# Sharing softmax exps between ScalarE and VectorE: lending a PSUM bank and waiting for full PV rounds in a planned attention kernel

## The chip, the cores and the metric

The kernel runs on one core of a Trainium2 chip. The metric is the device time of one execution in microseconds. Before the change three runs gave 832.87, 833.47 and 835.27 us, with a median of 833.47 us.

## What is computed

A layer norm of x (2048 rows, 512 wide) feeds multi-query attention with 32 heads of width 16, and beside it a two-matrix SiLU network of width 1792. The SiLU of the network's result gates the attention's result.

```python
xn = _layernorm(x)
q = (xn @ wq).reshape(B, S, 32, 16).transpose(0, 2, 1, 3)
k, v = xn @ wk, xn @ wv                       # one key and value head for all
scores = jnp.einsum("bhqd,bkd->bhqk", q, k) * 16 ** -0.5
o = jnp.einsum("bhqk,bkd->bhqd", softmax(scores), v)
s = o.transpose(0, 2, 1, 3).reshape(B, S, 512) @ wo
h = _silu(xn @ w1)                            # 512 -> 1792
return x + s * _silu(h @ w2)                  # 1792 -> 512
```

## The kernel before

The 2048 x 2048 scores of 32 heads make 2048 slots. A slot is one matmul on TensorE (PE in the profile): 128 keys by 512 queries of one head, into one PSUM bank. The slots are ordered by group `g`: 512 queries of four heads, 64 slots, 32 groups in all. Every slot's scores must go through an exp, and the result meets V in a PV matmul that adds to the bank `OB` of its group.

There are two ways through the exp.

- ScalarE (ACT): a unit of three slots (banks 0 to 2, the wide buffer) or of two (banks 3 and 4, the narrow buffer) is turned into bf16 by one ACTIVATE (L1130) into one of six `pa_sb` buffers. The two buffers take turns. One PV matmul per slot follows (`pa_sb`).
- VectorE (DVE): a slot is turned into bf16 bits by one linear TENSOR_SCALAR out of PSUM (L839, `db_sb`), an exp in which the mantissa is linear. Four such slots make a batch, and five more TENSOR_SCALARs over the whole batch (L871, `ds_sb`) add constants to the bits; the six shifted copies are weighted in V (`v_sb`) and added up by PV. So a DVE slot costs one eviction, five quarters of a shift, and six PV matmuls in place of one. The banks for DVE slots are 5 and 7 (`POOL_BANKS`), which also serve the projections (`jobs`: q, the network's h and z, and the output w; L390).

TensorE works in two modes. An S phase (`do_S`, L677) fills the next ACT unit and up to two DVE slots: two to four matmuls in different row strips that run at once. All else is in rounds: four matmuls into four column strips at once, either of a job or of PV (`do_pv`, L928). A PV round holds, for each of the four heads, one operand that is ready, and may have fewer than four matmuls.

All of it is put in order before the kernel runs, by a planner in the kernel's own code. It keeps a clock per engine and places instructions at planned costs: a round or an S phase takes `MM` = 216 ns, a change between the two modes `SWITCH` = 105 ns, an exp of n slots 0.8333 * 512 * n + 65 ns, an eviction 620 and a shift 600 ns, and there are fixed latencies between engines. The engines then run these orders as they are, each waiting on semaphores of the others. So a rule of the planner sets the order on every engine. The rules that matter here are:

- `want_d` and `dve_backlog`: an S phase takes DVE slots only while the planned DVE backlog is at most `DVE_LIMIT` = 2500 ns and a pool bank is free; at most one beside a wide unit, at most `D_MAX2` = 2 beside a narrow one.
- `s_phase_ready`: an S phase comes when the banks of the next unit are free; `pe_step` puts rounds in between only as far as they don't make the planned S phase too late for ACT (`act_need`, `S_TOL`).
- `pv_round`: a PV round is issued with whatever is ready.
- The order on DVE goes by priority: evictions have 2, shifts 6.

Of the kernel before, what the change touches and what calls it, by code (L numbers as in the profile page):

```python
# [5 lines left out]
ACT = mybir.ActivationFunctionType  # L6
ALU = mybir.AluOpType
# [14 lines left out]
SHIFT_BETA = -0.603400124  # L22
K = len(SHIFT)

PE, AC, DV, PO, SP, AQ = "PE", "ACT", "DVE", "POOL", "SP", "ACTQ"
ENGINES = (PE, AC, DV, PO, SP)
MM = 216.0
SWITCH = 105.0
INF = float("inf")
DVE_LIMIT = 2500.0  # L30
MARGIN, MARGIN_END = 16, 28
D_MAX2 = 2
S_TOL = 30.0


# [184 lines left out]
def bass_recurrent_scan__grouped_kv_mqa__dense_activation_silu__prompt_kernel(  # L220
# [27 lines left out]
    POOL_BANKS = (5, 7)  # L248
    NPA, NDB, NDS = 6, 4, 2 * (K - 1)
    NQR, NON = 4, 2 * NOC  # L250

    with ExitStack() as es:
# [35 lines left out]
        ps = es.enter_context(nc.psum_tensor([P, 8 * 512], FP32))  # L288
# [9 lines left out]
        pl = Planner()  # L298
# [59 lines left out]
        for j in range(4):  # L358
            a, b = 4 * j, 4 * j + 4
# [264 lines left out]
        nleft = [SLOTS] * NG  # L624
# [4 lines left out]
        st = dict(gA=0, gD=0, gO=0, fill=0, expn=0, assigned=0)  # L629
# [5 lines left out]
        pool_free = list(POOL_BANKS)  # L635
# [16 lines left out]
        def take(g, i):  # L652
            kt = left[g, i].pop(0)
            nleft[g] -= 1
            left_oct[g // 2] -= 1
            st["assigned"] += 1
            return kt
# [29 lines left out]
        def dve_backlog():  # L687
            return sum(t.dur for t in pl.tasks[DV] if all(p.op is not None for p in t.preds)) + max(0.0, pl.clk[DV] - pl.clk[PE])

        def want_d(banks_left=True):  # L690
            if st["assigned"] < 8 or not pool_free:
                return False
            if any(c not in evac_kt or evac_kt[c].op is None for c in range(NC)):
                return False
            if dve_backlog() > DVE_LIMIT:
                return False
            return True
# [39 lines left out]
        class Unit:  # L737
            pass

        def s_phase_ready():  # L740
            ub = st["fill"] % 2
            banks = A_BANKS[ub]
            if len(units) >= 2 and units[-2].exp is None:
                return None
            g = a_group(0)
            if g >= NG:
                return None
            if not all(slot_ok(g, i) for i in range(4) if left[g, i]):
                return None
            r = 0.0  # L750
            for b in banks:
                r = max(r, pl.ready(PE, (), [("ps", b)]))
            i = next(i for i in range(4) if left[g, i])
            r = max(r, pl.ready(PE, s_reads(g, i, left[g, i][0]), ()))
            return r
# [5 lines left out]
            return t  # L761

        def pe_start(t, mode):
            return t + (SWITCH if pl.mode not in (None, mode) else 0.0)

        def do_S(t):
            ub = st["fill"] % 2
            banks = A_BANKS[ub]
            dslots = []
            bt = None  # L770
            avoid = set()
            nd = 0
            if want_d():
                bt = d_batch()
                if bt is not None:
                    need = [i for i in range(4) if i not in bt.slots and left[bt.g, i] and slot_ok(bt.g, i)]
                    need.sort(key=lambda i: -len(left[bt.g, i]))
                    if need:
                        cap = len([b for b in pool_free if pl.ready(PE, (), [("ps", b)]) <= t + 30])
                        nd = min(cap, 4 - len(banks), len(need), 1 if len(banks) == 3 else D_MAX2)  # L780
                        for i in need[:nd]:
                            avoid.add(i)
                            dslots.append((bt.g, i, take(bt.g, i)))
            sl = pick_a(len(banks), avoid)
            if sl is None:
                for (g, i, kt) in dslots:
                    left[g, i].insert(0, kt)
                    nleft[g] += 1
                    left_oct[g // 2] += 1
                    st["assigned"] -= 1  # L790
                return False
            mm = []
            reads, writes = [], []
            for k, (g, i, kt) in enumerate(sl):
                mm.append((banks[k], g, i, kt))
                reads += s_reads(g, i, kt)
                writes.append(("ps", banks[k]))
            dinfo = []
            for (g, i, kt) in dslots:
                fb = [b for b in pool_free if pl.ready(PE, (), [("ps", b)]) <= t + 30]  # L800
                b = fb[0]
                pool_free.remove(b)
                mm.append((b, g, i, kt))
                reads += s_reads(g, i, kt)
                writes.append(("ps", b))
                dinfo.append((b, g, i, kt))
            seen = {}
            for (_, _, i, _) in mm:
                seen[i] = seen.get(i, 0) + 1
            dur = MM * max(seen.values())  # L810
            mm.sort(key=lambda m: 0)

            def emit(pe, mm=tuple(mm)):
                h = None
                for (b, g, i, kt) in mm:
                    h = s_mm(pe, b, g, i, kt)
                return h
            op = pl.place(PE, dur, emit, sorted(set(reads)), writes, t0=max(t, pe_start(pl.clk[PE], "S")))
            pl.mode = "S"
            u = Unit()  # L820
            u.slots, u.banks, u.exp, u.pv, u.s_end = sl, banks, None, len(sl), pl.vis(op, AC)
            u.idx = len(units)
            units.append(u)
            st["fill"] += 1
            for (g, i, kt) in sl:
                tot[g, i] += 1
            if dinfo:
                if not bt.slots:
                    batches.append(bt)
                    db_busy[bt.b] = 4  # L830
                for (b, g, i, kt) in dinfo:
                    bt.slots[i] = kt
                    tot[g, i] += K

                    def placed(pop, b=b, g=g, i=i, kt=kt, bt=bt):
                        pool_free.append(b)
                        pvq[g][i].append((pop, v_lhs(0 + 1, g, kt), db_sb[:, bt.b, i * NQ:(i + 1) * NQ].bitcast(BF16),
                                          [("Db", bt.b, i)] + v_reads(1, kt), ("b", bt)))
                    bt.P[i] = pl.add(Task(DV, 620.0, lambda v, b=b, i=i, bb=bt.b: v.tensor_scalar(  # L839
                        db_sb[:, bb, i * NQ:(i + 1) * NQ], bank(b), 128.0 * LOG2E, 128.0 * SHIFT_BETA + 16256.0,  # L840
                        op0=ALU.mult, op1=ALU.add), [("ps", b)], [("Db", bt.b, i)], 2, on_place=placed))
                if len(bt.slots) == 4:
                    make_shifts()
            return True
# [37 lines left out]
        def pv_round(t):  # L882
            g = st["gO"]
            if g >= NG:
                return None
            if g > 0 and norm.get(g - 1) is None or g > 0 and norm[g - 1].op is None:
                return None
            rb = pl.ready(PE, (), [("ps", OB)])
            if rb > t + 20:
                return ("wait", rb)  # L890
            got = {}
            soon = INF
            for i in range(4):
                for k, ent in enumerate(pvq[g][i]):
                    if ent[3][-1][1:] not in v_ready:
                        continue
                    r = max(pl.vis(ent[0], PE), pl.ready(PE, ent[3], ()))
                    if r <= t + 20:
                        got[i] = k
                        break  # L900
                    soon = min(soon, r)
            if not got:
                return ("wait", soon)
            return ("go", got)

        def do_pv(t, got):
# [156 lines left out]
        def a_pressure():  # L1063
            return sum(1 for b in pa_busy if b)

        def pe_step():
            t = pl.clk[PE]
# [6 lines left out]
            pr = pv_round(t)  # L1074
            tr = tail_round(t)
            col = None
            if pr and pr[0] == "go" and (a_pressure() >= NPA - 2):
                col = ("pv", pr[1])
            elif jr[0] == "go":
                col = ("job", jr[1])  # L1080
            elif pr and pr[0] == "go" and len(pr[1]) >= 3:
                col = ("pv", pr[1])
            elif pr and pr[0] == "go":
                col = ("pv", pr[1])
            elif tr and tr[0] == "go":
                col = ("tail", None)
            if ts is not None:
# [3 lines left out]
                elif col is not None:  # L1091
                    mode = col[1].mode if col[0] == "job" else "C"
# [138 lines left out]
```

## Time and profile before

| What | Value |
|---|---|
| median of three runs | 833.47 us |
| the profiled execution: its time, its span | 833.06 us, 831.3 us |
| ACT busy | 794.5 us, 96% of the span |
| PE busy | 723.5 us, 87% |
| DVE busy | 681.4 us, 82% |
| slots through ACT, through DVE | 1668, 380 |
| ACTIVATEs of three slots, of two | 334, 333 |

The span is from the first to the last instruction. Busy time counts an instant once, also where two instructions of an engine overlap. The chain of work that ended last is followed back from the last instruction, and says which engine the end hung on.

### The profile page before, as it was taken

What the parts mean: (1) busy time and instruction counts of PE and PEld (TensorE: products, weight loads), DVE (VectorE), ACT (ScalarE), POOL (GpSimd) and SP (SyncE); (2) the same over time, 40 slices, a digit from 0 to 9 for tenths busy, and PEclk for the clock granted to TensorE, in tenths of its full rate; (3) what the DMA queues carried; (4) which work ended last, traced back from release to release, by engine and by line L of the source; (5) the groups of instructions that cost most, each with busy time, mean ns of one, the idle gap of its engine ahead of it and who ended that gap; (6) DMA issues with size and microseconds to landing.
All of it is one profiled execution on the core that took longest, in us unless ns stands there. A gap on an engine that the chain in (4) does not pass through costs nothing.

```text
span 831.3 us, 19227 instructions
## 1 busy us (share of the span) xinstructions
PE 723.5 (87%) x8492; PEld 211.9 (25%) x8492; DVE 681.4 (82%) x1159; ACT 794.5 (96%) x743; POOL 17.2 (2%) x47
## 2 busy tenths in 40 slices
PE   3988888888988889999988989888989889898986
PEld 1422222222222222222222222222222222222221
DVE  7678887798797887989988878988878788888882
ACT  1999999999999999999999999999999999999994
POOL 2410000000000000000000000000000000000000
PEclk9999999999999999999999999999999999999988
DMA  9100000000000000000000000000000000000000
GB/s 317 39 14 1 2 2 2 1 2 2 2 1 14 27 15 1 2 2 2 2 1 3 26 26 2 2 1 2 2 2 1 14 27 14 1 2 2 2 1 26
DMA packets 11394, 12.53 MB, mean 15 GB/s; under 512 B 1776, under 2 KB 10736, under 8 KB 11312
## 3 DMA queue, kind: packets, MB, share of 16 engines
q1 hardware_dynamic: 9728, 10.75, 4.0%
q8 instruction: 67, 1.10, 0.5%
q10 hardware_dynamic: 1584, 0.56, 0.3%
q14 instruction: 15, 0.12, 0.0%
HBM read 8.95 MB, written 2.10 MB: 13 GB/s over the span
## 4 chain that ended last, share of the span: by engine, by line
ACT 86%; PE 8%; DVE 4%; POOL 1%; issue 1%; ACTq 0%; DVEq 0%
ACT pa_sb L1130 82%; ACT t_sb L505 3%; PE ps L390 3%; PE ps L928 2%; PE ps L677 2%; DVE ds_sb L871 1%; ACT t_sb L528 1%; DVE db_sb L839 1%; DVE v_sb L334 1%; DVE stats_sb L348 1%; DVE xn_sb L367 0%; PE ps L405 0%; POOL v_sb L462 0%; POOL rstd_sb L363 0%; DVE qt_sb L485 0%
## 5 line engine op out<-in xcount | busy, mean ns | idle before, releaser
L1130 ACT ACTIVATE pa_sb<-ps 128x1536 bf16<-128x1536 f32 (+1 forms) x667 | 782.6, 1475 | 10.6 <-PE ps L677 8.6
L677 PE MATMUL ps<-qt_sb,kt_sb 32*128 32x512 bf16 x2048 | 265.4, 390 | 79.0 <-ACT pa_sb L1130 72.8
L839 DVE TENSOR_SCALAR db_sb<-ps 128x512 uint16<-128x512 f32 x380 | 257.1, 684 | 93.3 <-PE ps L677 92.3
L871 DVE TENSOR_SCALAR ds_sb<-db_sb 128x2048 uint16<-128x2048 uint16 x475 | 307.1, 683 | 2.7
L928 PE MATMUL ps<-pa_sb,v_sb 128*32 128x512 bf16 x1668 | 256.2, 390 | 1.6 <-DVE f_sb L945 1.0
L928 PE MATMUL ps<-ds_sb,v_sb 128*32 128x512 bf16 x1900 | 229.3, 389 | 3.9 <-DVE ds_sb L871 2.3
L677 PEld LDWEIGHTS ps<-qt_sb,kt_sb 32*128 32x128 bf16 x2048 | 65.6, 91 | 345.3 <-ACT pa_sb L1130 318.9
L928 PE MATMUL ps<-db_sb,v_sb 128*32 128x512 bf16 x380 | 124.3, 390 | 2.7 <-DVE f_sb L945 2.3
L928 PEld LDWEIGHTS ps<-pa_sb,v_sb 128*32 128x32 bf16 x1668 | 65.4, 95 | 79.3 <-issue 56.3
L928 PEld LDWEIGHTS ps<-ds_sb,v_sb 128*32 128x32 bf16 x1900 | 58.7, 95 | 72.5 <-DVE ds_sb L871 34.9
L390 PE MATMUL ps<-w_sb,u_sb 128*32 128x512 bf16 x896 | 73.8, 384 | 0.1
L390 PE MATMUL ps<-xnT_sb,w_sb 128*32 128x512 bf16 x896 | 72.2, 388 | 0.5 <-DVE u_sb L507 0.5
L505 ACT ACTIVATE t_sb<-ps 128x512 bf16<-128x512 f32 x56 | 47.8, 853 | 0.0
L507 DVE SCALAR_TENSOR_TENSOR u_sb<-t_sb,ps 128x512 bf16<-128x512 bf16 x56 | 38.1, 681 | 10.3 <-ACT t_sb L505 9.9
L928 PEld LDWEIGHTS ps<-db_sb,v_sb 128*32 128x32 bf16 x380 | 31.0, 95 | 18.4 <-DVE f_sb L945 5.8
L945 DVE STREAM_TRANSPOSE f_sb<-ps 128x512 f32<-128x512 f32 x32 | 22.7, 708 | 15.0 <-PE ps L928 15.0
L390 PEld LDWEIGHTS ps<-xnT_sb,w_sb 128*32 128x32 bf16 x896 | 19.0, 95 | 29.8 <-issue 20.2
L390 PEld LDWEIGHTS ps<-w_sb,u_sb 128*32 128x32 bf16 x896 | 18.0, 94 | 29.0 <-issue 21.7
L390 PE MATMUL ps<-wo_sb,on_sb 128*32 128x512 bf16 x256 | 21.0, 424 | 0.5 <-DVE u_sb L507 0.5
L390 PE MATMUL ps<-xnT_sb,wq_sb 128*32 128x512 bf16 x256 | 20.4, 398 | 0.0
L405 PE MATMUL ps<-ident,xn_sb 128*128 128x128 bf16 x64 | 7.1, 289 | 12.8 <-DVE xn_sb L367 12.8
L485 DVE TENSOR_SCALAR qt_sb<-ps 128x512 bf16<-128x512 f32 x16 | 11.0, 688 | 6.6 <-PE ps L390 6.6
(39 smaller groups left out, 155.3 us busy)
## 6 DMA issues: line engine op xcount, KB each, us to landing
w_sb<-in_B_w_dram SPq DMA_DIRECT2D x2, 1792.0 KB, 14.0
xr_sb<-in_A_x_dram SPq DMA_DIRECT2D x16, 128.0 KB, 2.2
out_dram<-ob_sb SPq DMA_DIRECT2D x16, 128.0 KB, 1.7
ds_sb<-in_A_x_dram SPq DMA_DIRECT2D x3, 512.0 KB, 9.2
ds_sb<-in_A_x_dram SPq DMA_DIRECT2D x2, 256.0 KB, 3.3
wq_sb<-in_A_wq_dram ACTq DMA_DIRECT2D x1, 512.0 KB, 8.6
wo_sb<-in_A_wo_dram SPq DMA_DIRECT2D x1, 512.0 KB, 14.8
kt_sb<-kt_sb SPq DMA_DIRECT2D x4, 64.0 KB, 2.4
```

The costliest lines, as they stand in the source:

```text
L334: pl.add(Task(DV, 260.0, lambda v, j=j: v.memset(v_sb[:, j, :, :], 1.0 if j == 0 else SHIFT_W[j - 1]), (), [("V", j, c) for c in range(NC) ...
L348: pl.add(Task(DV, 593.0, lambda v, t=t: v.bn_stats(stats_sb[:, t, :], x_tile(t)), [xkey(t)], [("st", t)], 1 + j))
L390: last = h.matmul(bank(b)[32 * j:32 * (j + 1), :], lhsT=lhs(j), rhs=rhs, start=start, stop=stop, tile_position=(0, 32 * j), skip_group_che ...
L485: t = Task(DV, 620.0, lambda v: v.tensor_scalar(qt_sb[:, oi % NQR, :], bank(b), QSCALE, None, op0=ALU.mult), [("ps", b)], [("qT", oi % NQR ...
L505: t1 = Task(AC, 492.0, lambda a: a.activation(t_sb[:, k, :], bank(b), ACT.Tanh, scale=0.5), [("ps", b)], [("t", k)], 0)
L507: t2 = Task(DV, 620.0, lambda v: v.scalar_tensor_tensor(out=u_sb[:, ft, :], in0=t_sb[:, k, :], scalar=1.0, in1=bank(b), op0=ALU.add, op1=A ...
L677: return pe.matmul(bank(b), lhsT=kt_sb[32 * i:32 * i + 32, g % 2, kt * P:(kt + 1) * P], rhs=qt_sb[32 * i:32 * i + 32, (g // 2) % NQR, :], ...
L839: bt.P[i] = pl.add(Task(DV, 620.0, lambda v, b=b, i=i, bb=bt.b: v.tensor_scalar(db_sb[:, bb, i * NQ:(i + 1) * NQ], bank(b), 128.0 * LOG2E, ...
L871: pl.add(Task(DV, 600.0, lambda v, s=s, j=j, bb=bt.b: v.tensor_scalar(ds_sb[:, s, :], db_sb[:, bb, :], SHIFT[j], None, op0=ALU.add), [("Db ...
L928: h = pe.matmul(bank(OB)[32 * i:32 * (i + 1), :], lhsT=lhs, rhs=rhs, start=s0, stop=s1, tile_position=(0, 32 * i), skip_group_check=True)
L945: t1 = pl.add(Task(DV, 640.0, lambda v: v.transpose(f_sb[:, k, :], bank(OB)), [("ps", OB)], [("F", k)], 1, [norm.get(("m", g - 2))]))
L1130: op = pl.place(AC, 0.8333 * NQ * n + 65.0, lambda a: a.activation(pa_sb[:, s, 0:n * NQ], ps[:, b0 * 512:(b0 + n) * 512], ACT.Exp), [("ps" ...
```

## The change

The planner gets other rules; the operations themselves stay as they are.

- Beside a wide unit, an S phase may now take a second DVE slot, in the wide buffer's third bank, or a first one there where no pool bank is free. The ACT unit is then of two slots. This is done while the planned DVE backlog is below `LEND_LIMIT` = 3000 ns, and a second slot is wanted only below `TWO_LIMIT` = 1500 ns. A lent bank's eviction gets priority 0, and the wide buffer's next S phase waits for it. Beside a narrow unit two slots are taken below `TWO_LIMIT`, else one.
- `DVE_LIMIT` goes from 2500 to 4000 ns, and a free pool bank is no longer asked for at that point.
- A PV round of fewer than four matmuls is held for up to `HOLD` = 1000 ns after its oldest operand came, unless four of the six `pa_sb` buffers are taken, or the group has no slots left to give.
- The planner lets a mode change run during a wait: the start is the later of now and the last PE end plus `SWITCH`, where it was now plus `SWITCH`.

```diff
-DVE_LIMIT = 2500.0
+DVE_LIMIT = 4000.0
-D_MAX2 = 2
+LEND_LIMIT = 3000.0
+TWO_LIMIT = 1500.0
+HOLD = 1000.0
...
         def want_d(banks_left=True):
-            if st["assigned"] < 8 or not pool_free:
+            if st["assigned"] < 8:
...
         def s_phase_ready():
...
+            if lent.get(ub) is not None and lent[ub].op is None:
+                return None
...
         def pe_start(t, mode):
-            return t + (SWITCH if pl.mode not in (None, mode) else 0.0)
+            return max(t, pl.order[PE][-1].end + SWITCH if pl.mode not in (None, mode) else 0.0)
...
-                        nd = min(cap, 4 - len(banks), len(need), 1 if len(banks) == 3 else D_MAX2)
+                        bl = dve_backlog()
+                        want = 2 if bl < TWO_LIMIT else 1
+                        nd = min(cap, 4 - len(banks), len(need), want)
+                        if nd < min(want, len(need)) and len(banks) == 3 and bl < LEND_LIMIT:
+                            nd, lend = nd + 1, True
...
+            if lend:
+                banks, extra = banks[:2], banks[2]
             sl = pick_a(len(banks), avoid)
...
-                        op0=ALU.mult, op1=ALU.add), [("ps", b)], [("Db", bt.b, i)], 2, on_place=placed))
+                        op0=ALU.mult, op1=ALU.add), [("ps", b)], [("Db", bt.b, i)], 2 if b in POOL_BANKS else 0, on_place=placed))
+                    if b not in POOL_BANKS:
+                        lent[ub] = bt.P[i]
...
             if not got:
                 return ("wait", soon)
+            if len(got) < 4 and nleft[g] > 0 and t - old < HOLD and a_pressure() < NPA - 2:
+                return ("wait", min(soon, old + HOLD))
             return ("go", got)
```

What the new rules make of the order was counted in the two built programs:

| | before | after |
|---|---|---|
| slots through ACT, through DVE | 1668, 380 | 1596, 452 |
| ACTIVATEs of three slots, of two | 334, 333 | 222, 465 |
| DVE evictions, shifts | 380, 475 | 452, 565 |
| S phases on PE | 667 | 687 |
| PV matmuls | 3948 | 4308 |
| PV rounds | 1179 | 1132 |
| of them with four matmuls | 771 | 998 |

The programs' orders show it at three places, in the middle of the run. Line numbers of the changed kernel are some 20 higher: its exps are L1149, its evictions L855, its shifts L889, its S matmuls L679, its PV matmuls L949.

First ACT, at the 32nd and 33rd `t_sb` tanh (there are 72, of the jobs h and z). Before, around the 33rd:

```order
L1130 ACTIVATE pa_sb<-ps 128x1024
L1130 ACTIVATE pa_sb<-ps 128x1536
L528 ACTIVATE t_sb<-ps 128x512
L1130 ACTIVATE pa_sb<-ps 128x1024
L1130 ACTIVATE pa_sb<-ps 128x1536
```

After, from the 32nd on:

```order
L507 ACTIVATE t_sb<-ps 128x512
L1149 ACTIVATE pa_sb<-ps 128x1024 x4
L1149 ACTIVATE pa_sb<-ps 128x1536
L1149 ACTIVATE pa_sb<-ps 128x1024 x3
L1149 ACTIVATE pa_sb<-ps 128x1536
L1149 ACTIVATE pa_sb<-ps 128x1024
```

Where three-slot and two-slot exps took turns, there are now stretches of two-slot exps alone (x3, x4): in them the wide buffer's third bank is with DVE.

Second DVE, just behind the transpose that ends the 13th group. Before:

```order
L945 STREAM_TRANSPOSE f_sb<-ps 128x512
L871 TENSOR_SCALAR ds_sb<-db_sb 128x2048
L839 TENSOR_SCALAR db_sb<-ps 128x512
L948 RECIPROCAL rcp_sb<-f_sb 128x16
L871 TENSOR_SCALAR ds_sb<-db_sb 128x2048
L949 TENSOR_TENSOR otr_sb<-f_sb,rcp_sb 128x16x16
L839 TENSOR_SCALAR db_sb<-ps 128x512
```

After:

```order
L966 STREAM_TRANSPOSE f_sb<-ps 128x512
L855 TENSOR_SCALAR db_sb<-ps 128x512
L969 RECIPROCAL rcp_sb<-f_sb 128x16
L855 TENSOR_SCALAR db_sb<-ps 128x512
L970 TENSOR_TENSOR otr_sb<-f_sb,rcp_sb 128x16x16
L855 TENSOR_SCALAR db_sb<-ps 128x512
L889 TENSOR_SCALAR ds_sb<-db_sb 128x2048 x3
```

Evictions now stand between the steps of the norm where a shift stood before: more scores are waiting for DVE at that moment, and the shifts of the batch come behind them.

Third PE, near the middle of the run, from one S phase over the next three. Before:

```order
L677 MATMUL ps<-qt_sb,kt_sb 128x512 x4
L928 MATMUL ps<-pa_sb,v_sb 32x512 x3
L928 MATMUL ps<-db_sb,v_sb 32x512
L677 MATMUL ps<-qt_sb,kt_sb 128x512 x2
L928 MATMUL ps<-pa_sb,v_sb 32x512 x2
L928 MATMUL ps<-db_sb,v_sb 32x512
L677 MATMUL ps<-qt_sb,kt_sb 128x512 x4
```

After:

```order
L679 MATMUL ps<-qt_sb,kt_sb 128x512 x4
L949 MATMUL ps<-ds_sb,v_sb 32x512 x2
L949 MATMUL ps<-pa_sb,v_sb 32x512 x2
L949 MATMUL ps<-ds_sb,v_sb 32x512 x4
L679 MATMUL ps<-qt_sb,kt_sb 128x512 x2
L949 MATMUL ps<-ds_sb,v_sb 32x512 x8
L679 MATMUL ps<-qt_sb,kt_sb 128x512 x3
```

Between S phases stood rounds of three or four PV matmuls; now there are eight, two full rounds each, that draw on shifts of earlier batches.

More of the change, by code (lines that the diff above doesn't have):

```diff
@@ L23 @@
 K = len(SHIFT)
-PE, AC, DV, PO, SP, AQ = "PE", "ACT", "DVE", "POOL", "SP", "ACTQ"
+PE, AC, DV, PO, SP = "PE", "ACT", "DVE", "POOL", "SP"
 ENGINES = (PE, AC, DV, PO, SP)
@@ L738, in bass_recurrent_scan__grouped_kv_mqa__dense_activation_silu__prompt_kernel @@
             pass
+        lent = {}
         def s_phase_ready():
@@ L772, in do_S @@
             nd = 0
+            lend = False
             if want_d():
@@ L798, in do_S @@
             dinfo = []
[L799 to L802, printed above, removed]
+            for k, (g, i, kt) in enumerate(dslots):
+                lent_here = lend and k == len(dslots) - 1
+                if lent_here:
+                    b = extra
+                else:
+                    b = [b for b in pool_free if pl.ready(PE, (), [("ps", b)]) <= t + 30][0]
+                    pool_free.remove(b)
                 mm.append((b, g, i, kt))
@@ L810, in do_S @@
             dur = MM * max(seen.values())
-            mm.sort(key=lambda m: 0)
             def emit(pe, mm=tuple(mm)):
@@ L835, in placed @@
                     def placed(pop, b=b, g=g, i=i, kt=kt, bt=bt):
-                        pool_free.append(b)
+                        if b in POOL_BANKS:
+                            pool_free.append(b)
                         pvq[g][i].append((pop, v_lhs(0 + 1, g, kt), db_sb[:, bt.b, i * NQ:(i + 1) * NQ].bitcast(BF16),
@@ L891, in pv_round @@
             got = {}
-            soon = INF
+            soon, old = INF, INF
             for i in range(4):
@@ L899, in pv_round @@
                         got[i] = k
+                        old = min(old, r)
                         break
@@ L1080, in pe_step @@
                 col = ("job", jr[1])
-            elif pr and pr[0] == "go" and len(pr[1]) >= 3:
-                col = ("pv", pr[1])
             elif pr and pr[0] == "go":
```

## The prediction

> **What bounds the kernel now.** I read the page's head, busy times and chain first, then the busy times stage by stage, then the waits.
>
> ```profile
> span 831.3 us, 19227 instructions
> PE 723.5 (87%) x8492; PEld 211.9 (25%) x8492; DVE 681.4 (82%) x1159; ACT 794.5 (96%) x743; POOL 17.2 (2%) x47
> ...
> ACT 86%; PE 8%; DVE 4%; POOL 1%; issue 1%; ACTq 0%; DVEq 0%
> ```
>
> The end hangs on ACT. The profiled execution took 833.06 us, 1.8 more than its span and 0.4 below the median of the runs, so the sum is made against 831.3 and 1.8 is added at the end.
>
> ```profile
> core 0: us, PE busy (x) PEld busy (x) DVE busy (x) ACT busy (x) POOL busy (x), PEclk, DMA share, GB/s
> 40.00:320.00 280.00, 244.86 (x2972) 70.89 (x2964) 232.23 (x386) 280.00 (x267) 2.55 (x7) 1.00 0.02 6
> 320.00:480.00 160.00, 146.02 (x1731) 41.98 (x1731) 137.85 (x230) 159.66 (x150) 0.00 (x0) 1.00 0.02 6
> 480.00:560.00 80.00, 71.45 (x833) 20.20 (x830) 68.11 (x114) 77.10 (x73) 0.00 (x0) 0.96 0.02 6
> 560.00:680.00 120.00, 106.63 (x1269) 31.11 (x1269) 97.75 (x165) 120.00 (x115) 0.00 (x0) 1.00 0.02 6
> 680.00:800.00 120.00, 107.16 (x1232) 29.73 (x1224) 102.73 (x172) 118.03 (x109) 0.00 (x0) 0.96 0.02 6
> sum 760.00, PE 676.12 PEld 193.90 DVE 638.67 ACT 754.78 POOL 2.55; mean PE 135.22 PEld 38.78 DVE 127.73 ACT 150.96 POOL 0.51
> ```
>
> From 40 to 800 us ACT idles 760 − 754.78 = 5.2 us; nearly all of it falls where the granted clock is 0.96. DVE idles 121.3 us there (16%), PE 83.9 us. So ACT's own work is the bound, and DVE has room. The waits say what DVE lacks, and that ACT is hardly kept waiting:
>
> ```profile
> DVE db_sb L839 <- PE ps L677: 92.3, 121, 1.6
> DVE u_sb L507 <- ACT t_sb L505: 9.9, 14, 1.6
> ACT pa_sb L1130 <- PE ps L677: 8.6, 13, 2.5
> ...
> DVE tmp_sb L530 <- ACT t_sb L528: 3.1, 4, 1.4
> ```
>
> DVE waits 121 times for scores that no S phase has given it; ACT waits for S phases 13 times only.
>
> **What the change takes from ACT.** The price of an exp comes from pieces of the chain with four, five and six exps in a row, where wide and narrow take turns:
>
> ```profile
> 52.53 4.52 ACT pa_sb L1130 x4
> 57.54 5.44 ACT pa_sb L1130 x5
> 63.47 6.78 ACT pa_sb L1130 x6
> ```
>
> Four to five adds a narrow one, 0.92 us; five to six adds a wide one, 1.34 us. (The mean durations of single records are longer, since neighbours overlap.) The new order has 112 wide exps fewer and 132 narrow ones more: −112 × 1.34 + 132 × 0.92 = −150.1 + 121.4 = −28.7 us. All of it lies on the chain, so with ACT as busy as now the span would be 831.3 − 28.7 = 802.6 us.
>
> **What it adds to DVE.** 72 evictions and 90 shifts more. Their price:
>
> ```profile
> L871 DVE TENSOR_SCALAR ds_sb<-db_sb 128x2048 uint16<-128x2048 uint16 x475 | 307.1, 683 | 2.7
> L839 DVE TENSOR_SCALAR db_sb<-ps 128x512 uint16<-128x512 f32 x380 | 257.1, 684 | 93.3 <-PE ps L677 92.3
> 384.09 0.68 DVE L839 TENSOR_SCALAR db_sb<-ps 128x512 uint16<-128x512 f32 x1
> 384.69 0.68 DVE L871 TENSOR_SCALAR ds_sb<-db_sb 128x2048 uint16<-128x2048 uint16 x1
> 385.29 0.68 DVE L839 TENSOR_SCALAR db_sb<-ps 128x512 uint16<-128x512 f32 x1
> 387.87 1.90 DVE L871 TENSOR_SCALAR ds_sb<-db_sb 128x2048 uint16<-128x2048 uint16 x3
> ```
>
> One record lasts 0.68 us, but the next starts 0.60 us behind it, and three shifts take 1.90, that is (1.90 − 0.68) / 2 = 0.61 us a step. So one more in a full queue costs 0.61; the ends are 0.60 and 0.684. In the new order of DVE, four of the added instructions stand ahead of the first group's transpose and six behind the 31st's; the six fall into the tail, where DVE is idle today:
>
> ```profile
> 820.95 0.72 DVE L945 STREAM_TRANSPOSE f_sb<-ps 128x512 f32<-128x512 f32 x1 [10.82 <-PE ps L928]
> ```
>
> Six steps of 0.61 are 3.7 us, hidden under these 10.82. If the last shifts came later than the last exps, up to 3.7 would show at the end. The other 152 go into the middle: 152 × 0.61 = 92.7 us. DVE then has 638.67 + 92.7 = 731.4 us of work in a middle that ACT leaves at 760 − 28.7 = 731.3. The two engines are level, which is what decides this case: ACT's saving is there only if DVE idles hardly at all. By bounds: at 0.684 a step DVE has 742.6 us, 11.3 more than ACT; and since each of the 121 waits also ends a run of overlapping records, 0.08 us of drain a time is counted as busy now and is gone in a full queue, some 10 us, so the lower end is 722, 10 less.
>
> The Trainium skill (VectorE: DVE Perf Modes, section "The DRAIN you can't avoid") says that the next operation does not start until the pipe of the one before is empty. Read as the whole record it would put every added instruction at 0.68 us, and the sum at 831.3 − 28.7 + 11.3 = 813.9 before any wait; the rows above, with 0.60 from start to start under a record of 0.68, disagree.
>
> **What it adds to PE.** The rows of one S phase, three rounds and the next S phase:
>
> ```profile
> 385.62 0.40 PE L677 MATMUL ps<-qt_sb,kt_sb 32*128 32x512 bf16 x4 [0.24 <-ACT pa_sb L1130]
> 385.94 0.39 PE L928 MATMUL ps<-ds_sb,v_sb 128*32 128x512 bf16 x1
> 385.95 0.40 PE L928 MATMUL ps<-pa_sb,v_sb 128*32 128x512 bf16 x3
> 386.17 0.39 PE L928 MATMUL ps<-ds_sb,v_sb 128*32 128x512 bf16 x3
> 386.39 0.38 PE L928 MATMUL ps<-db_sb,v_sb 128*32 128x512 bf16 x1
> 386.70 0.39 PE L677 MATMUL ps<-qt_sb,kt_sb 32*128 32x512 bf16 x3
> ```
>
> From round to round 0.22 us; S phase to round 0.32 and the last round to the S phase 0.31, so an S phase costs 0.32 + 0.31 − 0.22 = 0.41. PE gets 20 S phases more (8.2 us) and 47 PV rounds fewer (−10.3): −2 us although there are 360 PV matmuls more, because 998 rounds are full where 771 were. PE's 676 us then stand in 731, 92% where it was 89%. The holding itself costs nothing as long as PE finds other work in that microsecond; its cover is the 84 us that PE idles. The planner's softer mode change moves only where it places a start; its effect is in these counts. Slots of ACT that are lent away need no DMA, and no queue is passed.
>
> **What new waits it makes.** The wide buffer's S phase now also waits for the lent bank's eviction, and behind that S phase stands all of PE, then ACT. From S phase to S phase of that buffer there are two narrow exps, 1.84 us; the eviction needs 0.68 and may find DVE inside another 0.6. That leaves half a microsecond for the two semaphores, so mostly it is hidden. Also, in a lent stretch both refills must fit under a narrow exp (0.92), where today one of the two lies under a wide one (1.34). That one refill under 0.92 works today:
>
> ```profile
> L1130 ACT ACTIVATE pa_sb<-ps 128x1536 bf16<-128x1536 f32 x118 | 203.9, 1728 | 0.4 <-PE ps L677 0.4
> ```
>
> Between 40 and 320 us, 118 wide exps whose scores were filled under a narrow one waited 0.4 us in all. But 0.92 − 0.41 leaves room for two rounds and 0.07 us.
>
> Bounds for what ACT loses to all this: 0 (it fits as today) and one round, 0.22 us, at each of the 121 wide units that are lent (343 of 687 units fill the wide buffer, 222 still have three slots), 26.6 us. It is nearest to today's rows, where lateness shows under the lower clock alone; I take today's 5.2 us once more, since twice as many refills are tight. For DVE I take +3: a quarter of the 13 us that it waits today for ACT's tanh (9.9 for h and 3.1 for z, above), since such a hole now adds straight to its full queue. Sum: 831.3 − 28.7 + 5.2 + 3 = 810.8 us span, and 1.8 outside: 812.6, so 812.
>
> **The rivals.**
>
> DVE becomes the bound, and it is slower. DVE would have to idle more than 760 − 731.4 = 28.6 us in the middle, 24% of today's 121.3. For it: DVE's order is fixed, 93 us of today's idling ended at an S phase, and a late eviction of a lent bank now stops PE and through it ACT, so that holes of one engine are passed to the others. Against: slots are given until the backlog stands at 4000 ns instead of 2500. If a third of the idling stays (40 us) the middle is 772 and the time 831.3 + 1.8 + 12 = 845.
>
> S phases come late in lent stretches. At 0.22 us for half of the 121 units it is 13.3 in place of 5.2: 821; for all of them 834, which is no change. The stretches of three and four narrow exps in the order speak for it, PE's idle time against it.
>
> DVE steps cost the whole record of 0.68 in a full queue: 11.3 us more than the level case, 824. The start-to-start row of 0.60 speaks against it, but from a few steps. (The skill's rule above is this one.)
>
> Nothing new is lost: the span is ACT's, 802.6 to 805.5, the time 804 to 807. That the change doesn't do what it says is ruled out by the counts.
>
> **How the numbers follow.** From no change a measurement here tells about 0.3%, 2.5 us. Forecast (807 to 817) 0.48; nothing lost (below 807) 0.08; late S phases up to 831, 0.18; steps of 0.68 0.06; these are faster, 0.80. Late S phases at their full price, 831 to 836, 0.07: the same. DVE the bound, above 836, 0.13. From 803 to 831 the range leaves these last two outside; it needs no more below, as ACT alone gives 804.
>
> **What would show it.** Two-slot exps 465 and three-slot ones 222 in the groups of L1149, with ACT busy near 765 us. DVE busy near 770, and its wait of 92 us for S matmuls down below 35. PE busy still near 722. If ACT's waits for PE grow beyond 20 us, S phases or lent banks are late: the releaser of those S matmuls tells which, ACT (a refill) or DVE (a lent bank). Wrong would be a DVE busy below 93% of the middle with ACT waiting too: then holes are passed around. And wrong the other way would be a step of DVE well under 0.60.

## The result, and the profile after

The changed kernel takes 805.21 us (median of four runs, 801.57 to 805.5) against 834.37 for the kernel before (median of four, now with one run of 840.31): a ratio of 0.9628, with a 95% interval from 0.9573 to 0.9683. Forecast were 812 us, within 803 to 831. The number comes out where the rival "nothing new is lost" stood, 804 to 807. The experiments show that this is not quite its mechanism: one part of the change, holding, takes back some of what the others bring, 4 to 8 us as it is counted below.

The profiled execution is the fastest of the four, 801.57 us. The page of the changed kernel, with the head, the busy times and the chain:

```profile
span 799.8 us, 20305 instructions
PE 717.5 (90%) x8852; PEld 205.9 (26%) x8852; DVE 760.7 (95%) x1321; ACT 764.7 (96%) x763; POOL 18.0 (2%) x47
...
ACT 80%; PE 11%; DVE 7%; POOL 1%; issue 1%; ACTq 0%; DVEq 0%
```

ACT still carries the end and is busy for the same 96%, of a shorter span. DVE went from 82% to 95%. The same stages as before the change, the last one cut where the run now nears its end (768 us), with busy times of PE, its weight loads, DVE, ACT and POOL, then the granted clock:

```profile
40.00:320.00 280.00, 257.13 (x3211) 72.56 (x3207) 271.71 (x462) 279.78 (x285) 3.35 (x7) 1.00 0.02 6
320.00:480.00 160.00, 148.72 (x1872) 42.35 (x1864) 158.35 (x272) 158.24 (x159) 0.00 (x0) 1.00 0.03 8
480.00:560.00 80.00, 73.32 (x924) 20.19 (x917) 77.97 (x135) 79.87 (x80) 0.00 (x0) 1.00 0.01 2
560.00:680.00 120.00, 111.56 (x1362) 31.13 (x1362) 115.73 (x200) 118.21 (x123) 0.00 (x0) 0.97 0.03 10
680.00:768.00 88.00, 81.43 (x1006) 22.84 (x1002) 87.49 (x150) 87.74 (x87) 0.00 (x0) 1.00 0.01 2
sum 728.00, PE 672.16 PEld 189.07 DVE 711.24 ACT 723.84 POOL 3.35; mean PE 134.43 PEld 37.81 DVE 142.25 ACT 144.77 POOL 0.67
```

In these 728 us ACT idles 4.2 us, DVE 16.8 (121.3 before), PE 55.8 (83.9 before). The waits that answer to those shown of before:

```profile
DVE db_sb L855 <- PE ps L679: 12.5, 29, 1.1
ACT pa_sb L1149 <- PE ps L679: 6.0, 6, 2.3
```

DVE's wait for scores fell from 92.3 us in 121 times to 12.5 in 29; ACT's wait for S phases did not grow (8.6 before).

### The profile page after: what moved, and what is told of

Read it like the earlier page. It is cut to its first block, busy times and chain, and to the rows that moved or that the text cites. A ratio compares the mean times of both kernels' runs of the same rounds, so it can differ in the third digit from the quotient of the medians.

```text
span 799.8 us, 20305 instructions
## 1 busy us (share of the span) xinstructions
PE 717.5 (90%) x8852; PEld 205.9 (26%) x8852; DVE 760.7 (95%) x1321; ACT 764.7 (96%) x763; POOL 18.0 (2%) x47
## 4 chain that ended last, share of the span: by engine, by line
ACT 80%; PE 11%; DVE 7%; POOL 1%; issue 1%; ACTq 0%; DVEq 0%
ACT pa_sb L1149 76%; PE ps L949 4%; PE ps L392 4%; PE ps L679 3%; ACT t_sb L507 3%; DVE ds_sb L889 2%; DVE db_sb L855 2%; ACT t_sb L530 1%; DVE stats_sb L350 1%; DVE xn_sb L369 1%; DVE v_sb L336 1%; POOL rstd_sb L365 0%; POOL v_sb L464 0%; DVE xnT_sb L418 0%; DVE qt_sb L487 0%
## 5 line engine op out<-in xcount | busy, mean ns | idle before, releaser
L1149 ACT ACTIVATE pa_sb<-ps 128x1024 bf16<-128x1024 f32 (+1 forms) x687 | 750.0, 1365 | 7.9 <-PE ps L679 6.0
L889 DVE TENSOR_SCALAR ds_sb<-db_sb 128x2048 uint16<-128x2048 uint16 x565 | 366.3, 681 | 0.9
L679 PE MATMUL ps<-qt_sb,kt_sb 32*128 32x512 bf16 x2048 | 271.1, 387 | 56.6 <-ACT pa_sb L1149 46.0
L855 DVE TENSOR_SCALAR db_sb<-ps 128x512 uint16<-128x512 f32 x452 | 301.0, 682 | 14.7 <-PE ps L679 12.5
L949 PE MATMUL ps<-ds_sb,v_sb 128*32 128x512 bf16 x2260 | 290.8, 386 | 1.7 <-DVE ds_sb L889 1.1
L949 PE MATMUL ps<-pa_sb,v_sb 128*32 128x512 bf16 x1596 | 265.5, 389 | 1.9 <-DVE ds_sb L889 0.8
L679 PEld LDWEIGHTS ps<-qt_sb,kt_sb 32*128 32x128 bf16 x2048 | 68.5, 91 | 345.6 <-ACT pa_sb L1149 295.5
L949 PE MATMUL ps<-db_sb,v_sb 128*32 128x512 bf16 x452 | 128.2, 391 | 1.9 <-DVE f_sb L966 1.4
L949 PEld LDWEIGHTS ps<-ds_sb,v_sb 128*32 128x32 bf16 x2260 | 74.1, 95 | 69.9 <-issue 34.4
L949 PEld LDWEIGHTS ps<-pa_sb,v_sb 128*32 128x32 bf16 x1596 | 66.4, 95 | 58.0 <-issue 34.7
L392 PE MATMUL ps<-xnT_sb,w_sb 128*32 128x512 bf16 x896 | 75.6, 385 | 0.0
L507 ACT ACTIVATE t_sb<-ps 128x512 bf16<-128x512 f32 x56 | 46.4, 829 | 0.0
L949 PEld LDWEIGHTS ps<-db_sb,v_sb 128*32 128x32 bf16 x452 | 31.4, 95 | 17.9 <-issue 7.5
L530 ACT ACTIVATE t_sb<-ps 128x512 bf16<-128x512 f32 x16 | 12.1, 756 | 1.4 <-PE ps L392 1.4
```

The costliest lines, as they stand in the source:

```text
L392: last = h.matmul(bank(b)[32 * j:32 * (j + 1), :], lhsT=lhs(j), rhs=rhs, start=start, stop=stop, tile_position=(0, 32 * j), skip_group_che ...
L507: t1 = Task(AC, 492.0, lambda a: a.activation(t_sb[:, k, :], bank(b), ACT.Tanh, scale=0.5), [("ps", b)], [("t", k)], 0)
L530: t1 = Task(AC, 492.0, lambda a: a.activation(t_sb[:, k, :], bank(b), ACT.Tanh, scale=0.25), [("ps", b)], [("t", k)], 0)
L679: return pe.matmul(bank(b), lhsT=kt_sb[32 * i:32 * i + 32, g % 2, kt * P:(kt + 1) * P], rhs=qt_sb[32 * i:32 * i + 32, (g // 2) % NQR, :], ...
L889: pl.add(Task(DV, 600.0, lambda v, s=s, j=j, bb=bt.b: v.tensor_scalar(ds_sb[:, s, :], db_sb[:, bb, :], SHIFT[j], None, op0=ALU.add), [("Db ...
L949: h = pe.matmul(bank(OB)[32 * i:32 * (i + 1), :], lhsT=lhs, rhs=rhs, start=s0, stop=s1, tile_position=(0, 32 * i), skip_group_check=True)
```

## The experiments

All times are medians of four to ten runs, each with the kernel before on the same chip (834.4 us beside the changed kernel, 833.5 to 833.9 beside the others). "Clock" is the median of the runs' mean granted TensorE clock; that of the kernel before was 0.98.

| Kernel | time, us | ratio to before (95% interval) | clock |
|---|---|---|---|
| changed kernel | 805.2 | 0.9628 (0.9573 to 0.9683) | 0.982 |
| changed, without holding | 797.4 | 0.9582 (0.9550 to 0.9615) | 0.997 |
| changed, without lending | 829.0 | 0.9961 (0.9931 to 0.9990) | 0.978 |
| changed, old mode switch | 808.9 | 0.9714 (0.9679 to 0.9749) | 0.989 |
| before, with DVE_LIMIT 4000 | 821.0 | 0.9863 (0.9824 to 0.9901) | 0.984 |
| changed, both limits 4000 | 827.4 | 0.9933 (0.9908 to 0.9958) | 0.985 |
| changed, shifts cut up | 806.4 | 0.9674 (0.9648 to 0.9701) | 0.983 |
| changed, shorter exps | 786.1 | 0.9425 (0.9384 to 0.9466) | 0.986 |
| before, with holding | 837.6 | 1.0038 (1.0012 to 1.0064) | 0.970 |
| before, with fillers | 826.4 | 0.9912 (0.9890 to 0.9934) | 0.993 |
| changed, with fillers | 803.2 | 0.9642 (0.9622 to 0.9663) | 0.996 |
| changed, without holding, with fillers | 800.9 | 0.9606 (0.9587 to 0.9626) | 1.000 |
| changed, without holding, DVE_LIMIT 5000 | 813.8 | 0.9765 (0.9745 to 0.9786) | 0.989 |

### Which engine bounds it: shorter exps, and shifts cut up, in the same order

Two kernels keep the order of the changed one, and alter what an instruction costs behind the planner's back.

```diff
+                w = n * NQ - (64 if cover[s] >= n * NQ else 0)
...
-                    pa_sb[:, s, 0:n * NQ], ps[:, b0 * 512:(b0 + n) * 512], ACT.Exp),
+                    pa_sb[:, s, 0:w], ps[:, b0 * 512:b0 * 512 + w], ACT.Exp),
```

> The changed kernel with the same order, in which nearly every exp leaves out its last 64 columns (their old contents stay in the buffer): 64 x 0.83 ns x 680 exps = 36 us less on ACT, nothing else changed. Theory A: time falls until DVE is full, by about the 17 us that DVE idles in the middle: 788 us, with DVE busy over 97% of the middle. Rival P (PE, with 56 us of idle time cut up in small pieces, is as near): falls by under 8 us, with ACT waiting for S phases whose releaser is not DVE. Rival D (DVE is already level): no fall beyond 3 us.

Measured: 786.1 us, 19 less than the changed kernel, where theory A had 17. (`cover` is how much of a buffer has been written.) The middle of this kernel:

```profile
sum 708.00, PE 666.28 PEld 190.21 DVE 699.40 ACT 694.06 POOL 3.51; mean PE 666.28 PEld 190.21 DVE 699.40 ACT 694.06 POOL 3.51
```

DVE is busy for 699.4 of 708 us (98.8%) and ACT now idles 13.9. So ACT is the bound of the changed kernel, and DVE the next, less than 20 us below it.

```diff
+                        cuts = (0, 1024, 2048) if j <= 2 else (0, 2048)
+                        for lo, hi in zip(cuts, cuts[1:]):
+                            h = v.tensor_scalar(ds_sb[:, s, lo:hi], db_sb[:, bb, lo:hi], SHIFT[j], None, op0=ALU.add)
```

> The changed kernel with the same order, in which two of the five shifts of a batch are issued as two halves of 1024 columns each: 226 instructions more on DVE, at an estimated 0.33 us a half against 0.60 a whole some 14 us, that the planner doesn't know of. Theory A (ACT bounds, DVE's 17 us of idle time are free room): under 3 us more, up to 808 us. Rival D (DVE and ACT are level, and holes of one are passed to the other): 10 to 14 us more, 815 to 819 us.

Measured: 806.4 us, 1.2 more in medians (4 by the ratios, with intervals that overlap); at one clock, 0.988, a run of this kernel took 803.9 and one of the changed kernel 801.6. Half shifts follow each other every 0.336 us in the trace, so two cost 0.07 more than a whole one, 16 us for the 226. DVE's busy time in the whole run:

```profile
PE 720.6 (90%) x8852; PEld 207.7 (26%) x8852; DVE 771.1 (96%) x1547; ACT 765.5 (95%) x763; POOL 17.8 (2%) x47
```

10 us more than 760.7, since some runs of overlapping records now join. The time moved by 1 to 4 us, not by the 10 to 14 of rival D: the room is real, and holes are mostly not passed on, as theory A says.

### Which rule pays: parts left out, or done alone

```diff
-LEND_LIMIT = 3000.0
+LEND_LIMIT = -1.0
```

> The changed kernel with no lending of the third bank (LEND_LIMIT below zero); all else of the change stays. 1644 slots in 658 ACTIVATEs on ACT, 404 slots on DVE. Theory A: ACT has 743.1 us instead of 725.3, 17.8 more: 823 us, that is 10.8 us or a good third of the gain is left. Rival D (DVE holes set the time in the changed kernel): with 48 evictions and 60 shifts less DVE has much room, and the loss is smaller: 815 us or less.

```diff
-DVE_LIMIT = 2500.0
+DVE_LIMIT = 4000.0
```

> The kernel before with DVE_LIMIT = 4000 alone. The order happens to have the same split as the changed kernel without lending (1644 slots in 658 ACTIVATEs, 404 slots on DVE) but 1194 PV rounds instead of 1111. Theory A: 10.8 us of ACT less than before, 822.7 us, the same as without lending within 3 us. Rival P: without full rounds PE is late more often: 828 us or more, and clearly slower than the changed kernel without lending.

By the price of ACT's work both had to give 823. The higher limit alone gave 821.0, as theory A has it. The changed kernel without lending gave 829.0, outside both theories of its own run, and 8 us slower than the other at the very same split of the slots, with separate intervals. It even has 83 PV rounds fewer. What sets the two apart is holding, the planning of mode switches, the pool bank that is no longer asked for, and the choice of one or two slots beside a narrow unit (`TWO_LIMIT` for `D_MAX2`). ACT's waits in the kernel without lending, and in the one with the limit alone:

```profile
ACT pa_sb L1149 <- PE ps L949: 9.5, 7, 2.6
ACT pa_sb L1149 <- PE ps L679: 6.9, 10, 2.3
```

```profile
ACT pa_sb L1130 <- PE ps L677: 6.0, 8, 2.5
ACT pa_sb L1130 <- PE ps L928: 2.8, 3, 1.4
```

Most of the gap is in the waits for PV matmuls (L949, L928), 9.5 us against 2.8; all of them stand at the end of a group, of which more below. The clock explains little of it: at 0.988 the kernel without lending took 826.6 us, and at 0.989 the one with the limit alone 819.4 and 819.8. Which of the four rules makes these waits wasn't tested.

```diff
-HOLD = 1000.0
+HOLD = 0.0
```

> The changed kernel with HOLD = 0: partial PV rounds are issued at once. The order has 1234 PV rounds instead of 1132, and nearly the same exps (1592 slots in 683 ACTIVATEs instead of 1596 in 687), 456 slots on DVE instead of 452. Theory A (time is ACT's work, priced at 0.42 us a slot and 0.08 an ACTIVATE, and today's small losses): ACT has 2.0 us less, so about 803 us against 805 of the changed kernel. Rival P (the gain needs the full rounds, since PE has little room): 102 rounds of 0.22 us are 22 us more on a PE that idles some 56 us in the middle, and S phases come late: 812 us or more, with ACT waiting for PE.

Measured: 797.4 us, and no single run (797.3 to 800.4) as slow as the fastest of the changed kernel's four. By the ratios the gap is smaller, 0.5% or 4 us, and the two intervals overlap; 2 us of it were expected from ACT's work. Rival P had the sign wrong: with 102 PV rounds more it is faster. Theory A's 803 is missed by 6 too. PE is busier, and the granted clock is full in nearly the whole run:

```profile
PE 724.9 (91%) x8872; PEld 212.9 (27%) x8872; DVE 766.9 (96%) x1330; ACT 762.2 (96%) x759; POOL 17.2 (2%) x47
...
PEclk9999999999999999999999999999999999999999
```

```diff
-            return max(t, pl.order[PE][-1].end + SWITCH if pl.mode not in (None, mode) else 0.0)
+            return t + (SWITCH if pl.mode not in (None, mode) else 0.0)
```

> The changed kernel with the old planning of mode switches. The order gives DVE 468 slots instead of 452, ACT 1580 slots in 685 ACTIVATEs. Theory A: ACT has 6.9 us less, so 798 us unless the order itself makes ACT wait; DVE gets 16 evictions and 20 shifts more, 22 us against 17 us that it idles in the middle, so some of it comes back: 798 to 803 us. Rival D (DVE is the bound as it is): 805 + 22 x 0.5 or more, 812 us and above. Rival S (planned starts that are later than they need be make S phases late): ACT waits of 10 us or more, 808 us.

Measured: 808.9, the number of rival S. The order has 6.9 us less of ACT's work than the changed kernel, but ACT waits 17.9 us for PE in it:

```profile
ACT pa_sb L1149 <- PE ps L949: 9.0, 11, 1.5
ACT pa_sb L1149 <- PE ps L679: 8.9, 8, 2.3
```

Half of it is for PV matmuls (L949), at the ends of groups again. Of the 8.9 us for S phases 4.8 fall in the first 40 us, and of the rest all but 0.2 at half clock (see below). So the new planning of mode switches goes with a gain of a few microseconds, though it gives DVE fewer slots. Rival S's mechanism, late planned starts, isn't shown.

### What holding does: the clock

```diff
             if not got:
                 return ("wait", soon)
+            if len(got) < 4 and nleft[g] > 0 and t - old < 1000.0 and a_pressure() < NPA - 2:
+                return ("wait", min(soon, old + 1000.0))
             return ("go", got)
```

> The kernel before with the holding of partial PV rounds alone. The split is the old one (1668 slots in 667 ACTIVATEs, 380 on DVE), and PV rounds fall from 1179 to 1079, 22 us of PE. Theory A: no change, within 2 us of the kernel before. Rival P (PE's lateness is part of what ACT loses): 2 to 5 us faster than before, the 5 us that ACT idles in the middle.

Measured: slower by 0.4%, at a clock of 0.970. With the split unchanged, neither theory has a loss. The clock is the trail. The traces record it as stretches of 3.41 us, or whole multiples, at half speed. One of them in the kernel before, at 489 us: four-microsecond stretches (PE busy with instructions, weight loads, DVE, ACT, POOL; then the clock), PE's rows and ACT's.

```profile
484.00:488.00 4.00, 3.20 (x39) 0.95 (x36) 1.64 (x4) 4.00 (x5) 0.00 (x0) 1.00 0.00 0
488.00:492.00 4.00, 3.47 (x32) 0.81 (x30) 3.39 (x6) 3.82 (x4) 0.00 (x0) 0.63 0.02 4
492.00:496.00 4.00, 4.00 (x56) 1.13 (x56) 3.47 (x7) 3.27 (x5) 0.00 (x0) 0.94 0.20 66
```

```profile
487.43 0.40 PE L677 MATMUL ps<-qt_sb,kt_sb 32*128 32x512 bf16 x4 [0.78 <-ACT pa_sb L1130]
488.68 0.39 PE L677 MATMUL ps<-qt_sb,kt_sb 32*128 32x512 bf16 x3 [0.53 <-ACT pa_sb L1130]
490.41 0.61 PE L677 MATMUL ps<-qt_sb,kt_sb 32*128 32x512 bf16 x3
```

```profile
491.06 1.02 ACT L1130 ACTIVATE pa_sb<-ps 128x1024 bf16<-128x1024 f32 x1 [0.18 <-PE ps L677]
492.82 2.36 ACT L1130 ACTIVATE pa_sb<-ps 128x1536 bf16<-128x1536 f32 x2 [0.73 <-PE ps L677]
```

Ahead of it PE ran out of rounds and idled 0.78 and 0.53 us; then the clock halves, matmul records grow from 0.39 to 0.61 us, and ACT, which waits nowhere else between 484 and 500 us, waits 0.18 and 0.73 us for S phases. From 40 us on, all nine of ACT's waits for S phases in the kernel before, and all four in the changed kernel, lie in such a stretch or up to 3 us behind it; the kernel without holding has no such stretch and no such wait between 40 and 792 us.

Over the profiles of all 14 kernels, each 3.41 us window at full clock (from 36 us on, without the last 20) was set against the window behind it. PE counts as streaming for 0.213 us from the start of each matmul:

| share of the window in which PE streams | windows | followed by half clock |
|---|---|---|
| below 0.39 | 23 | 23 |
| 0.39 to 0.42 | 15 | 9 |
| 0.42 to 0.46 | 53 | 4 |
| 0.46 and more | over 2900 | 0 |

Holding packs PE's work into fewer rounds with longer idle time between them, and more windows fall below 0.42: 8 with holding added against 5 before, 2 in the changed kernel against none without holding. In the middle of the run, half-clock stretches add up to 20 us before, 34 with holding added, 14 in the changed kernel (in the profile, its run with the highest clock), and none in the one without holding. To test that this costs time, the fillers add work to PE and leave the orders of ACT and DVE as they are but for a few places:

```diff
+            if ts is not None and g < NG and "zz" in pl.lastw and pe_start(t, "C") + MM + SWITCH <= ts:
+                strips = [i for i in range(4) if 0 < done[g, i] and (nleft[g] > 0 or done[g, i] < tot[g, i])]
...
+                            h = pe.matmul(bank(OB)[32 * i:32 * (i + 1), :], lhsT=zz_sb[:, 0:32], rhs=wq_sb[:, 0, :],
+                                          start=False, stop=False, tile_position=(0, 32 * i), skip_group_check=True)
```

> The kernel before, with filler rounds: where the planner finds PE idle long enough ahead of the next S phase, it places a round of four matmuls with zero weights that adds zero to the open PV bank. 262 of them, some 57 us more work on PE; the split of the slots stays at 1668 in 667 ACTIVATEs and 380 on DVE. In the profiles so far, the granted clock falls to half for 3.41 us whenever PE was streaming for less than some 42% of the 3.41 us ahead. Theory C (these half-clock stretches make S phases late, and cost 0.7 to 1 us each): the stretches in the middle go, mean clock 0.993 or more instead of 0.98, and the time falls by 4 to 7 us to 827 to 830 although work is only added. Rival A (ACT's work alone): no change within 2 us. Rival P (more work on PE makes S phases late): slower, 836 us or more.

Measured: 826.4 us, 7 less than before, at a clock of 0.993, with PE's busy time up by 36 us and the numbers of instructions on ACT and DVE as they were. That is theory C, 0.6 us beyond its range, and shows that the clock's stretches cost the kernel before about 0.9% of its time.

```profile
PE 760.0 (92%) x9514; PEld 231.4 (28%) x9514; DVE 680.5 (83%) x1159; ACT 793.4 (96%) x743; POOL 17.2 (2%) x48
```

> The changed kernel with its holding of partial rounds, and with the same filler rounds (263). 1592 slots in 681 ACTIVATEs, 456 on DVE, as good as the run without holding (1592 in 683, 456). Theory C (holding costs what it costs through the clock, since it packs PE's work into fewer rounds and leaves idle windows): clock 0.993 or more, 796 to 799 us, level with the run without holding. Rival H (holding costs by itself, since it delays PV and so pa buffers and the norm): 803 us or more, whatever the clock.

> The changed kernel without holding and with filler rounds (163). Its clock is 0.996 already without filler. Theory C: no change within 2 us, 796 to 799. Rival P (fillers get in the way of S phases): 800 us or more.

Measured: 803.2 with holding, 800.9 without, with clocks of 0.996 and 1.000. Between the two the gap is 2 us in medians, where without fillers it was 8, but 3 and 4 by the ratios, so these two kernels alone don't settle what holding costs by itself. And theory C in its pure form fails twice: with fillers the kernel with holding does not come down to 797, and the one without holding loses 3.5 us by them. Fillers thus also get in the way: ACT's waits for PV matmuls are 7.7 us in the profile of the kernel without holding and with fillers, 5.1 without them. ACT's waits in the kernel with holding and fillers point to PV as well, not to S phases:

```profile
ACT pa_sb L1163 <- PE ps L951: 6.3, 5, 3.1
ACT pa_sb L1163 <- PE ps L681: 3.4, 2, 2.3
```

The single runs tell more. The clock also differs between runs of one kernel, and the time goes with it: over the 37 runs of the kernel before that stand beside the experiments, it rises by some 0.4 us for each 0.001 of clock lost. At one clock, holding costs nothing that can be seen. On the same chip the kernel before with holding took 833.4 us at 0.983 and 837.5 to 838.1 at 0.969, the kernel before 832.3 to 833.0 and 838.5. With fillers, the one run with holding at a clock of 1.000 took 800.6 us, those without 801.4 and 801.6. The changed kernel and the one without holding never ran at one clock; at 0.4 to 0.6 us per 0.001, the former's 801.6 at 0.988 would be 799 to 800 at 0.992 (an estimate), where the latter took 800.4. So in these three pairs holding costs what its clock costs. In the kernel without lending, where the gap stands at one clock too, that isn't so, or another rule is at fault.

### Where more DVE slots stop paying

```diff
-LEND_LIMIT = 3000.0
-TWO_LIMIT = 1500.0
+LEND_LIMIT = 4000.0
+TWO_LIMIT = 4000.0
```

> The changed kernel with both limits at 4000 ns (LEND_LIMIT, TWO_LIMIT), so that two DVE slots are taken wherever slots are given at all: 480 slots on DVE (480 evictions, 600 shifts), 1568 slots in 714 ACTIVATEs on ACT. ACT's work falls by another 9.6 us, DVE's grows by 63 x 0.60 = 38 us, more than the 17 us that it idles in the middle. Theory A with a full DVE: ACT alone would give 795.6, DVE needs 728 + 38 - 17 = 749 us in the middle instead of 728 if it is to do all of that there: 812 to 826 us. Rival (DVE's holes and drains shrink again as they did from before to after, 18 us): 797 to 803 us.

The last kernel leaves holding out and sets `DVE_LIMIT` to 5000.

> The changed kernel without holding and with DVE_LIMIT = 5000: 464 slots on DVE, 1584 slots in 673 ACTIVATEs on ACT, 4.2 us of ACT's work less than without holding alone, and 11 us of DVE's more, about what DVE idles there in the middle (11.7). Theory A: 794 to 797 us. Rival D (DVE is full and passes holes on): 799 to 806 us, with ACT waiting 5 us more.

Measured: 827.4, and 813.8. Both are above what was expected for a full DVE, by 1 us over its 812 to 826 and by 8 us over its 799 to 806; the theories with 794 to 803 fall. The middle of the first:

```profile
sum 750.00, PE 691.86 PEld 195.90 DVE 742.08 ACT 713.42 POOL 2.86; mean PE 691.86 PEld 195.90 DVE 742.08 ACT 713.42 POOL 2.86
```

DVE is busy for 98.9%, and ACT idles 36.6 us. How a full DVE reaches ACT is in its waits (both limits at 4000 first, then the limit of 5000) and in the rows around one of them in the first, at 229 us, far from any half clock:

```profile
ACT pa_sb L1149 <- PE ps L949: 30.3, 18, 3.0
```

```profile
ACT pa_sb L1149 <- PE ps L949: 17.4, 12, 2.9
```

```profile
223.19 3.09 DVE L889 TENSOR_SCALAR ds_sb<-db_sb 128x2048 uint16<-128x2048 uint16 x5
...
225.79 0.40 PE L949 MATMUL ps<-ds_sb,v_sb 128*32 128x512 bf16 x4
226.20 0.68 DVE L509 SCALAR_TENSOR_TENSOR u_sb<-t_sb,ps 128x512 bf16<-128x512 bf16 x1
226.79 0.69 DVE L855 TENSOR_SCALAR db_sb<-ps 128x512 uint16<-128x512 f32 x1
227.40 0.71 DVE L966 STREAM_TRANSPOSE f_sb<-ps 128x512 f32<-128x512 f32 x1
...
228.16 0.39 PE L949 MATMUL ps<-pa_sb,v_sb 128*32 128x512 bf16 x1 [1.97 <-DVE f_sb L966]
...
228.82 1.02 ACT L1149 ACTIVATE pa_sb<-ps 128x1024 bf16<-128x1024 f32 x1 [2.95 <-PE ps L949]
```

It is not the lent bank. DVE does its shifts back to back, and the group's last PV round, at 225.79, comes right behind the fourth of these five, which ends near 225.7. The group's transpose then stands behind a fifth shift, a step of the network and an eviction in DVE's order, and starts at 227.40. PV of the next group uses the same bank and cannot start before the transpose is done, at 228.16; that group's exps meanwhile fill the `pa_sb` buffers, and ACT stands still for 2.95 us until a PV matmul frees one. All 30 such waits of the two kernels begin within 2 us of a group's transpose. In both kernels DVE has more work in the middle than ACT, 742 us against 713 and 727 against 721, as in the kernel with the old mode switch (727 against 720); in the changed kernel it is 711 against 724, and without holding 712 against 718.

## Why the prediction was right, and where it was not

**ACT's saving, −28.7 us.** Right: ACT's busy time fell by 29.8 us, and the medians by 29.2. The price of 0.92 and 1.34 us an exp also gave the kernel with the higher limit alone (823 against 821.0). ACT as the bound was shown by the shorter exps.

**DVE, 731.4 us against ACT's 731.3.** Too high: 711 of 728 us were used. The step is 0.601 us in the median, not 0.61, and the prediction kept its lower bound out of the sum: 0.08 us of drain goes with each hole. DVE had some 280 holes in the middle before and 100 after, so some 14 us of its busy time were drains that vanished. That leaves 638.7 + 152 × 0.601 − 14 = 716; what the other 5 us are stays open. The rival by the Trainium skill's rule (VectorE: DVE Perf Modes, section "The DRAIN you can't avoid"), read as 0.68 us a step and 824, is out by that step of 0.601. The term of +3 us for holes did not come: DVE's waits for ACT's tanh, 13.0 us before, are 1.3 in the changed kernel.

**S phases that come late, +5.2 us.** Mis-sized: ACT idles 4.2 us in the middle, where the 5.2 of before were to double. Lent stretches, with both refills under a narrow exp, are no problem; the lent bank is none either. What made S phases late before was the half clock, which the prediction saw ("nearly all of it falls where the granted clock is 0.96") and took as given.

**"The holding itself costs nothing as long as PE finds other work in that microsecond".** This step failed. Its cover, PE's idle time, is what the clock goes by in the table above: holding costs the changed kernel 8 us in medians (4 by the ratios, not clear of noise), and 0.4%, clear of noise, when it is added to the kernel before. At one clock that cost is gone. The prediction counted the 47 PV rounds fewer as −10.3 us of PE's work, −2 with the added S phases, of no use to a bound on ACT; they were a loss. That the time lies within the range is in part luck: the terms for late S phases and for holes, 8 us together, did not come, and without the loss by holding, which the sum has at nothing, the kernel took 797.4 us, below the 803 of the range.

**The rivals.** "DVE becomes the bound" needed DVE to idle more than 28.6 us in the middle; it idled 16.8. The two kernels with more DVE slots show such a bound by another way than the prediction's, which had late evictions of lent banks in mind: the group's end comes late, ACT stops for want of `pa_sb` buffers, and the time goes up by 16 to 22 us.

**What would show it.** 465 and 222 exps, ACT near 765 (764.7), DVE near 770 (760.7), its wait below 35 (12.5), PE near 722 (717.5): right.

The gain by parts, in medians: the higher limit alone 13 us, lending and the rest without holding another 24, holding 8 back. By the ratios holding's part is 4. The best kernel that computes every exp is the changed one without holding, 797.4 us.

## What to carry to other kernels

Price a transfer of work between engines by the increments of the bounding engine's chain, and ask how much of the other engine's busy time is drain that goes when its holes close. Before saving work on an engine that isn't the bound, look at what its idle time triggers: here packing TensorE's rounds halved its clock for microseconds at a time, and unneeded matmuls made the kernel before faster, though they cost time where the clock was full already. Give a helper engine no more work than the engine that it relieves has left: past that, its lateness at a group's end stops the other.

## What the runs showed of the hardware

In these 14 profiles, half-clock stretches of 3.41 us follow a 3.41 us window in which TensorE streams for less than some 42% of the time, always below 39%, never above 46%, as tabled above. No idle gap of that length is needed: in the middle of these 14 runs the longest distance between two matmul starts is 2.4 us. The Trainium skill (TensorE: Matmul & The Clock Gate, section "HAM oscillation — how this bites in real kernels") asks for no idle gaps of more than about 3.4 us; the window's length agrees with the 3.41 us here, the condition does not, and the measurement decides. In the 13 runs of the kernel before beside the first four kernels, the clock ranged from 0.985 to 0.975, and the time with it from 830.2 us to between 833.9 and 835.8, so differences between runs of one kernel go with it too.
